# Two chunks of attention's output in one bank, two banks for the state's increment, and expert loads issued in parts

## The chip, the cores and the metric

The kernel runs on one core of one Trainium2 chip. A core has a matrix engine (PE), a vector engine (DVE), a scalar engine (ACT), a general engine (POOL) and an engine that issues loads and stores (SP); each works through its own queue in order, and semaphores tie them together. The metric is the device time of one execution in microseconds (us). Matrix products land in the banks of PSUM; DVE and ACT read them from there.

## The reference

Three layers follow one another for 2 sequences of 768 tokens, all in fp32:

```python
for t in range(S):                                   # attention: 8 heads of 64
    state = gamma * state + einsum('bhd,bhe->bhde', k[:, :, t], v[:, :, t])
    y[:, :, t] = scale * einsum('bhd,bhde->bhe', q[:, :, t], state)
# a feed-forward layer, 512 -> 1024 -> 512
h = maximum(x @ w_in, 0)
c = sum over k in 0..2 of conv_w[k] * h shifted by k - 1 tokens
x = (h * sigmoid(c)) @ w_out
# mixture of experts: 8 experts, one for each token
e = argmax(x @ w_gate) or, where sigmoid(x @ w_local) >= 0.5, the expert of the token before
out = softmax(x @ w_gate)[e] * (maximum(x @ w1[e], 0) @ w2[e])
```

The weights `w_in`, `conv_w` and `w_out` arrive as 64-bit words and are narrowed on the chip.

## The kernel before

**Attention** works on pairs of heads (8 of them, `Head`) and chunks of 128 tokens (6 for each pair), 48 iterations in one loop (lines 427 to 450). In iteration i, `scores(i)` issues PE's product of k and q (L282, bank `s`, two of them) and DVE's multiplication with the decay mask (L284, `at`). Then `output(i - 2)` issues, for an older chunk: PE's `inc`, k transposed times v (L290, bank `i`, one of them); DVE's update of the state from it, in two halves (L295 for the first chunk of a head, L297 for the others, `st`); PE's result `y` (bank `y`, two of them) from two products with `at` (L300) and one with the state that the chunk before left (L302); and ACT's copy of `y` to its high part (L304). The low part, y minus high part, is DVE's (L305); it is returned as a function and issued one iteration later. High and low part are what later products read (`xT`), since a product in fp32 is made of three (`mm3`, lines 133 to 135).

Beside it run generators that `advance()` moves on once an iteration. `convert` narrows and splits one piece of 512 columns of `w_in` or `w_out`; its part `narrow` issues DVE's L149 and L150, ACT's L151, and two steps later POOL's addition L153. The number that a generator yields is the number of iterations until it goes on. ACT's L174 and POOL's or DVE's L176 then split the narrowed piece. `prepare` gets the next head ready: ACT copies q into `qz` (L253) and v into `vz` (L277), POOL scales q (L256). From iteration 25 on the loop also issues slices of `ffn_in` (L133 to L135, `h_ps`), and `hidden` (L350 to L363) follows each of its eight blocks.

The pools of this stage hold eight tiles, each in a bank of its own: `lg` one, `s` two, `i` one, `y` two, and one each for the weights' transposes and `h_ps`. The tile in bank `lg` is called `idle` until the logits begin: `keep_busy` lets PE write there before any data has come.

**The feed-forward layer** goes on with `ffn_in` for both sequences and `ffn_out`, which stores each tile of 128 tokens to `xs` in DRAM (L491, issued by SP). For the second sequence it does so in 20 units (lines 771 to 783), two or four of them for a tile; between them stand steps of the routing (`route`, `tables`) and the first loads of the experts.

**The experts** begin with `experts` (line 934). `fetch(j, which)` loads one expert's `w1` or `w2`, 2 MB in four parts, into `r` (L698); the expert's number is read by SP from `ei`. `fetch_q` does the same for a group of four quarter tiles, one part for each of four experts (L708, `qc` and `qs1l`). `gather` lets POOL collect the 128 tokens of one tile from `xs` (L727); the first two of these read only the tiles that were stored by unit 12, and the rest comes from `LAST`. `cut` splits the loaded weights on ACT (L717) and DVE (L718), and `begin_x` transposes the gathered tokens on PE (L813).

Of the kernel before, what the change touches and what calls it, by code (L numbers as in the profile page):

```python
# [9 lines left out]
F32 = mybir.dt.float32  # L10
F32R = mybir.dt.float32r
I32 = mybir.dt.int32
U32 = mybir.dt.uint32
AF = mybir.ActivationFunctionType
# [9 lines left out]
P = 128  # L24
CH = 128
# [66 lines left out]
def tile_kernel(ctx, tc, cat, cst, qT, kT, kN, vN, w_in, conv_w, w_out, wg, w1, w2, out):  # L92
    nc = tc.nc
    te, ve, se, po, sy = nc.tensor, nc.vector, nc.scalar, nc.gpsimd, nc.sync
    ctx.enter_context(tc.manual_schedule())

    def pool(name, bufs, stack=ctx, **kw):
        return stack.enter_context(tc.tile_pool(name=name, bufs=bufs, reuse_waits="tile", **kw))
# [16 lines left out]
    ps1 = pool("ps1", 2, ps_stack, space=PSUM)  # L115
# [30 lines left out]
    def narrow(words, n):  # L146
        lo, hi = words
        a = p1.tile([P, 512], I32, tag="na", name="na", bufs=4)[:, 0:n]
        ve.tensor_scalar(out=a, in0=hi, scalar1=3, scalar2=0x3FFFFFF8, op0=ALU.logical_shift_left, op1=ALU.bitwise_and)  # L149
        ve.scalar_tensor_tensor(out=a, in0=hi, scalar=-0x40000000, in1=a, op0=ALU.bitwise_and, op1=ALU.bitwise_or)  # L150
        se.activation(out=lo, in_=lo.bitcast(U32), func=AF.Copy, scale=2.0 ** -29)  # L151
        yield 2
        po.tensor_tensor(out=a, in0=a, in1=lo, op=ALU.add)  # L153
        yield 2
        return a.bitcast(F32)
# [4 lines left out]
    def convert(src, hi, lo, m=None):  # L160
# [8 lines left out]
        while slices[0] < GATES.get(m, 0):  # L169
            yield 1  # L170
        held.append(src)
        w = yield from narrow(words, 512)
        loaded.pop()
        se.activation(out=hi, in_=w, func=AF.Copy)  # L174
# [31 lines left out]
    idle = psl.tile([P, NG, 32], F32, name="lg").rearrange("p t n -> p (t n)")  # L206
# [14 lines left out]
    class Head:  # L221
# [64 lines left out]
        def output(self, c):  # L286
            at = self.at.pop(c)
            if c + 1 < NCH:
                inc = ps1.tile([P, P], F32, tag="i", name="inc", bufs=1)
                te.matmul(inc, self.kv[:, 0, c, :], self.kv[:, 1, c, :], start=True, stop=True)  # L290
                old, new = self.st[c % 2], self.st[(c + 1) % 2]
                for j in range(2):
                    pj = slice(64 * j, 64 * j + 64)
                    if c == 0:
                        ve.tensor_copy(out=new[pj, pj], in_=inc[pj, pj])  # L295
                    else:
                        ve.scalar_tensor_tensor(out=new[pj, pj], in0=old[pj, pj], scalar=self.g[j] ** CH, in1=inc[pj, pj], op0=ALU.mult, op1=ALU.add)  # L297
            y = ps1.tile([P, CH], F32, tag="y", name="y")
            for j in range(2):
                te.matmul(y, vz[:, c, j, :], at[:, j, :], start=(j == 0), stop=(c == 0 and j == 1))  # L300
            if c > 0:
                te.matmul(y, self.st[c % 2], self.q1[:, c, :], start=False, stop=True)  # L302
            hi, lo = (self.x[:, i, c * CH:(c + 1) * CH] for i in range(2))
            se.activation(out=hi, in_=y, func=AF.Copy)  # L304
            return lambda: ve.tensor_tensor(out=lo, in0=y, in1=hi.bitcast(F32), op=ALU.subtract)  # L305

# [93 lines left out]
    parts = [(w_in[:, i, j:j + 512], wi_hi[:, i, j:j + 512], wi_lo[:, i, j:j + 512]) for j in (0, 512) for i in range(4)]  # L400
# [26 lines left out]
    for i in range(len(seq) + LOOK):  # L427
        if i < len(seq):
            p, c = seq[i]
# [12 lines left out]
        if i >= LOOK:  # L442
            p, c = seq[i - LOOK]
# [30 lines left out]
    def ffn_out(b, t, ms):  # L474

        ts = slice(t * P, (t + 1) * P)
        if ms[0] == 0:
            OUT[b, t] = psb.tile([P, DM], F32, tag="x2", name="x2_ps")
        ps = OUT[b, t]
        for m in ms:  # L480
            g = hg[b, m]
            mm3(ps, g[:, 0, ts], g[:, 1, ts], wo_hi[:, m, :], wo_lo[:, m, :], m == 0, m == 7)
        if ms[-1] == 7:
            if b == B - 1 and t >= NG - 2:
                xn = xpool[0].tile([P, DM], F32, name=f"xl{t}", bufs=1)
                LAST.append(xn)
            else:
                xn = rt.tile([P, DM], F32, name="xn", bufs=2)
            se.activation(out=xn, in_=OUT.pop((b, t)), func=AF.Copy)
            r = b * S + t * P  # L490
            sy.dma_start(out=xs[r:r + P, :], in_=xn)  # L491
# [179 lines left out]
    QSLOT = ["c4", "s1l"]  # L671
    ncut, nq = [0], [0]
    W, QW = {}, {}

    def home(tag):
        return big if tag[0] == "s" else ws if tag == "c4" else wx

    def expert_at(n):
        return sy.value_load(ei[0:1, 0, n:n + 1], min_val=0, max_val=E - 1)

    def raw(lane, which):
        if (lane, which) not in RAW:
            RAW[lane, which] = (wx if lane and which else ws).tile([P, 4, 1024], F32, name=f"r{lane}{which}")
        return RAW[lane, which]

    def fetch(j, which):

        src = (w1, w2)[which].rearrange("e p a n -> e p (a n)")
        kw = {}
        if j == 0:  # L690
            src = src[0]
        else:
            src = src[bass.ds(expert_at(j), 1)].rearrange("o p n -> (o p) n")
            if j > 1:
                kw = dict(cond=sy.value_load(ei[0:1, 1, j:j + 1], min_val=0, max_val=1), cond_hint=True)
        dst = raw(j % 2, which)
        for i in range(4):
            sy.dma_start(out=dst[:, i, :], in_=src[:, i * 1024:(i + 1) * 1024], **kw)  # L698

    def fetch_q(g, which, i):  # L700

        tag = QSLOT[nq[0] % 2]
        nq[0] += 1
        QW[g, which, i] = w = home(tag).tile([P, 4, 1024], F32, tag=tag, name="q" + tag)
        src = (w1, w2)[which].rearrange("e p a n -> e p (a n)")
        for u in range(4):
            one_e = src[bass.ds(expert_at(NTILE + 4 * g + u), 1)].rearrange("o p n -> (o p) n")
            sy.dma_start(out=w[:, u, :], in_=one_e[:, i * 1024:(i + 1) * 1024])  # L708

# [13 lines left out]
    def gather(j, n=NT):  # L723

        X[j] = xg = xpool[0].tile([P, DM], F32, name="xg")
        po.memset(xg, 0.0)
        return po.indirect_dma_start(out=xg, out_offset=None, in_=xs[0:n], in_offset=bass.IndirectOffsetOnAxis(ap=it[:, j:j + 1], axis=0),  # L727
                                     bounds_check=n - 1, oob_is_err=False)
# [43 lines left out]
    for n, (t, ms) in enumerate(units, 1):  # L772
        ffn_out(1, t, ms)
        for step in STEPS.get(n, ()):
            next(step, done)
        if n == 8:
            fetch(1, 0)
        if n in (10, 14):
            cut(0, 0, n // 14)
        if n == 13:  # L780
            fetch_q(0, 0, 0)
            for j in range(2):
                gather(j, NT - 2 * P)
    p2_stack.close()
    q_stack.close()
    lg_stack.close()
# [276 lines left out]
```

## Time and profile before

| | us |
|---|---|
| median of 3 runs | 431.09 |
| lowest and highest | 430.42, 433.47 |
| the profiled execution | 429.99 |
| its span, first to last instruction | 428.2 |

| engine | busy us | share of the span |
|---|---|---|
| PE | 407.2 | 95% |
| DVE | 289.5 | 68% |
| ACT | 259.1 | 61% |
| POOL | 90.8 | 21% |

The profile is one execution. A group of instructions has a line number, the engine, the operation, what it writes and reads, its shape and count; then its busy time in us and the mean length of one in ns; then the idle time of its engine just before its instructions, with what ended that idle time. PEld is PE's loading of weights, which runs ahead of the products. An entry in order of time starts with its start and its length in us. The ends of PE's products are modelled, because they are pipelined.

### The profile page before, as it was taken

The page shows a single profiled execution, that of the slowest core. Times are in us where ns is not written, and L with a number is a line of the kernel's source. Part 1 is how long each engine was busy: PE and PEld are TensorE (multiplying, and loading weights), DVE is VectorE, ACT ScalarE, POOL GpSimd, SP SyncE. Part 2 cuts the span into 40 slices and gives each one's busy share as a digit, 9 for nine tenths or more (in the row PEclk, how much of TensorE's full clock was granted, in tenths as well). Part 3 has the DMA queues.
Part 4 walks back from the last instruction along what each step waited for, and adds up shares of the span by engine and source line. Part 5 has one row for each costly group of instructions (what it writes and reads, how often), then busy time and mean ns, then how long its engine had stood idle before and what let it go on. Part 6 is the DMA issues. An engine that isn't in the chain of part 4 may idle for free.

```text
span 428.2 us, 7291 instructions
## 1 busy us (share of the span) xinstructions
PE 407.2 (95%) x2412; PEld 328.1 (77%) x2412; DVE 289.5 (68%) x518; ACT 259.1 (61%) x429; POOL 90.8 (21%) x92
## 2 busy tenths in 40 slices
PE   8798899999999999999999999999999999999992
PEld 7697898888898778988768876767748676776881
DVE  4588879877976350477889058968663796858650
ACT  2677777658765212566704176869555786958560
POOL 5156655121110000000000330305212132111210
PEclk9899999999999999999999999999999999999997
DMA  7969773321000101000297799999979999684001
GB/s 232 389 229 392 280 248 104 100 59 41 2 0 2 49 27 48 26 0 2 64 377 277 280 342 373 346 413 410 396 285 338 404 375 366 248 280 186 25 22 51
DMA packets 27324, 86.59 MB, mean 202 GB/s; under 512 B 3598, under 2 KB 4622, under 8 KB 27280
## 3 DMA queue, kind: packets, MB, share of 16 engines
q1 hardware_dynamic: 25200, 79.76, 50.7%
q0 software_dynamic: 2080, 6.29, 3.8%
q8 instruction: 21, 0.34, 0.3%
q14 instruction: 23, 0.19, 0.1%
HBM read 105.18 MB, written 6.55 MB: 261 GB/s over the span
## 4 chain that ended last, share of the span: by engine, by line
PE 40%; issue 26%; DMA 16%; DVE 11%; ACT 3%; POOL 2%; SPq 1%; POOLq 0%; DVEq 0%; ACTq 0%
DMA out_dram<-yo,it 14%; PE h_ps L133 6%; PE h_ps L134 5%; PE h_ps L135 5%; PE x_ps L133 4%; PE y L300 3%; PE x_ps L135 3%; PE x_ps L134 3%; PE s_ps L282 3%; PE wc_ps L193 2%; PE inc L290 2%; DMA kq<-in_qT_dram 2%; PE lg L344 1%; PE y L302 1%; DVE cc L353 1%
## 5 line engine op out<-in xcount | busy, mean ns | idle before, releaser
L133 PE MATMUL h_ps<-xT,wih 128*128 128x384 f32 x128 | 46.6, 364 | 0.0
L353 DVE SCALAR_TENSOR_TENSOR cc<-h,cw,cc 128x768 f32<-128x768 f32 x32 | 34.3, 1072 | 16.8 <-ACT cc L350 16.7
L863 POOL DMA_INDIRECT out_dram<-yo,it x13 | 16.7, 1282 | 135.2 <-ACT yo L862 135.2
L727 POOL DMA_INDIRECT xg<-xs,it x13 | 18.8, 1443 | 120.8 <-DMA qc<-in_w_dram 112.2
L134 PE MATMUL h_ps<-xT,wih 128*128 128x384 f32 x128 | 43.1, 336 | 0.0
L135 PE MATMUL h_ps<-xT,wil 128*128 128x384 f32 x128 | 43.0, 336 | 0.0
L133 PE MATMUL x_ps<-woh,hg 128*128 128x512 f32 x96 | 38.5, 401 | 0.0
L134 PE MATMUL x_ps<-wol,hg 128*128 128x512 f32 x96 | 37.5, 391 | 0.0
L135 PE MATMUL x_ps<-woh,hg 128*128 128x512 f32 x96 | 37.5, 390 | 0.0
L718 DVE TENSOR_TENSOR ws0l<-r,ws0l 128x1024 fp32r<-128x1024 f32 x22 | 26.0, 1222 | 15.9 <-ACT ws0l L717 15.8
L300 PE MATMUL y<-at,vz 128*128 128x128 f32 x192 | 31.2, 285 | 1.8 <-ACT vz L277 0.9
L153 POOL TENSOR_TENSOR na<-na,raw 128x512 int32<-128x512 int32 (+1 forms) x17 | 21.2, 1250 | 49.3 <-ACT raw L151 19.3
L718 DVE TENSOR_TENSOR ws0h<-r,ws0h 128x1024 fp32r<-128x1024 f32 x22 | 26.0, 1222 | 8.3 <-ACT ws0h L717 6.1
L718 DVE TENSOR_TENSOR wc<-r,wc 128x1024 fp32r<-128x1024 f32 x22 | 26.0, 1221 | 8.2 <-ACT wc L717 8.2
L717 ACT ACTIVATE ws0l<-r 128x1024 fp32r<-128x1024 f32 x22 | 22.1, 1052 | 13.7 <-PE y L135 13.7
L282 PE MATMUL s_ps<-qz,kq 128*128 128x256 f32 x96 | 29.1, 386 | 1.0 <-DVE qz L251 1.0
L718 DVE TENSOR_TENSOR ws1h<-r,ws1h 128x1024 fp32r<-128x1024 f32 x22 | 26.0, 1222 | 6.0 <-ACT ws1h L717 4.0
L300 PEld LDWEIGHTS y<-at,vz 128*128 128x128 f32 x192 | 25.9, 195 | 4.3 <-DVE xT L305 2.3
L717 ACT ACTIVATE wc<-r 128x1024 fp32r<-128x1024 f32 x22 | 22.1, 1054 | 11.5 <-PE g L135 11.5
L284 DVE TENSOR_TENSOR at<-s_ps,ca 128x256 f32<-128x256 f32 x48 | 20.2, 420 | 12.3 <-PE s_ps L282 12.2
L133 PEld LDWEIGHTS h_ps<-xT,wih 128*128 128x128 f32 x128 | 24.1, 189 | 3.1 <-issue 1.8
L304 ACT ACTIVATE xT<-y 128x128 fp32r<-128x128 f32 x48 | 13.2, 274 | 20.9 <-PE y L302 19.0
(231 smaller groups left out, 1035.0 us busy)
## 6 DMA issues: line engine op xcount, KB each, us to landing
r<-in_w_dram SPq DMA_DIRECT2D x88, 512.0 KB
qc<-in_w_dram SPq DMA_DIRECT2D x32, 512.0 KB
qs1l<-in_w_dram SPq DMA_DIRECT2D x32, 512.0 KB
raw<-in_w_in_dram SPq DMA_DIRECT2D x8, 512.0 KB
raw<-in_w_out_dram SPq DMA_DIRECT2D x8, 512.0 KB
kq<-in_qT_dram SPq DMA_DIRECT2D x7, 384.0 KB
kq<-in_kT_dram SPq DMA_DIRECT2D x7, 384.0 KB
kv<-in_vN_dram SPq DMA_DIRECT2D x7, 384.0 KB
```

What stands on the lines that cost most here:

```text
L133: te.matmul(ps, lhi, rhi, start=first, stop=False)
L134: te.matmul(ps, lhi, rlo, start=False, stop=False)
L135: te.matmul(ps, llo, rhi, start=False, stop=last)
L153: po.tensor_tensor(out=a, in0=a, in1=lo, op=ALU.add)
L282: te.matmul(ps, self.kq[:, 0, tok], self.qz[:, :, tok], start=True, stop=True)
L284: ve.tensor_tensor(out=self.at[c], in0=ps, in1=self.dm, op=ALU.mult)
L300: te.matmul(y, vz[:, c, j, :], at[:, j, :], start=(j == 0), stop=(c == 0 and j == 1))
L353: ve.scalar_tensor_tensor(out=cc, in0=h[:, i:i + S], scalar=cw[:, m, i:i + 1], in1=cc, op0=ALU.mult, op1=ALU.add)
L717: se.activation(out=w[:, 0, h, :], in_=r, func=AF.Copy)
L718: ve.tensor_tensor(out=w[:, 1, h, :], in0=r, in1=w[:, 0, h, :].bitcast(F32), op=ALU.subtract)
L727: return po.indirect_dma_start(out=xg, out_offset=None, in_=xs[0:n], in_offset=bass.IndirectOffsetOnAxis(ap=it[:, j:j + 1], axis=0), bound ...
L863: po.indirect_dma_start(out=out, out_offset=bass.IndirectOffsetOnAxis(ap=it[:, j:j + 1], axis=0), in_=yo, in_offset=None, bounds_check=NT ...
```

## The change

Attention's `y` becomes a tile for two chunks. The even chunk writes the first half and returns; the odd one writes the second half, and ACT's and DVE's cuts are then made once for both, 256 columns each. There are still two such banks. The increment `inc` of odd chunks goes to the `idle` bank, that of even chunks to bank `i` as before. In `narrow`, ACT's instruction is issued right after L149, and DVE's second one (L150) an iteration later than the first; the POOL addition stays two iterations after the first. `fetch` and `fetch_q` take the parts to load as an argument: the load of the second tile's `w1` is issued as two parts after unit 8 and two after unit 12 (before: four after unit 8), and the first quarter load as three parts after unit 13, behind the first two gathers, and one after unit 16 (before: four after unit 13, ahead of the gathers in the program).

```diff
@@ narrow
         ve.tensor_scalar(out=a, in0=hi, scalar1=3, scalar2=0x3FFFFFF8, op0=ALU.logical_shift_left, op1=ALU.bitwise_and)
+        se.activation(out=lo, in_=lo.bitcast(U32), func=AF.Copy, scale=2.0 ** -29)
+        yield 1
         ve.scalar_tensor_tensor(out=a, in0=hi, scalar=-0x40000000, in1=a, op0=ALU.bitwise_and, op1=ALU.bitwise_or)
-        se.activation(out=lo, in_=lo.bitcast(U32), func=AF.Copy, scale=2.0 ** -29)
-        yield 2
+        yield 1
         po.tensor_tensor(out=a, in0=a, in1=lo, op=ALU.add)
@@ Head.output
-                inc = ps1.tile([P, P], F32, tag="i", name="inc", bufs=1)
+                inc = idle[:, 0:P] if c % 2 else ps1.tile([P, P], F32, tag="i", name="inc", bufs=1)
...
-            y = ps1.tile([P, CH], F32, tag="y", name="y")
+            if c % 2 == 0:
+                self.y = ps1.tile([P, 2, CH], F32, tag="y", name="y")
+            y = self.y[:, c % 2, :]
...
-            hi, lo = (self.x[:, i, c * CH:(c + 1) * CH] for i in range(2))
+            if c % 2 == 0:
+                return None
+            y = self.y.rearrange("p c t -> p (c t)")
+            hi, lo = (self.x[:, i, (c - 1) * CH:(c + 1) * CH] for i in range(2))
             se.activation(out=hi, in_=y, func=AF.Copy)
             return lambda: ve.tensor_tensor(out=lo, in0=y, in1=hi.bitcast(F32), op=ALU.subtract)
@@ fetch, fetch_q
-    def fetch(j, which):
+    def fetch(j, which, parts=range(4)):
...
-        for i in range(4):
+        for i in parts:
...
-    def fetch_q(g, which, i):
+    def fetch_q(g, which, i, parts=range(4)):
...
-        for u in range(4):
+        for u in parts:
@@ the units of the second sequence
-        if n == 8:
-            fetch(1, 0)
+        if n in (8, 12):
+            fetch(1, 0, range(2) if n == 8 else range(2, 4))
         if n in (10, 14):
             cut(0, 0, n // 14)
         if n == 13:
-            fetch_q(0, 0, 0)
             for j in range(2):
                 gather(j, NT - 2 * P)
+        if n in (13, 16):
+            fetch_q(0, 0, 0, range(3) if n == 13 else range(3, 4))
```

## Rows read from the trace of the kernel before

**Rows 1.** The page, part 1: busy us, share of the span, instructions.

```profile
PE 407.2 (95%) x2412; PEld 328.1 (77%) x2412; DVE 289.5 (68%) x518; ACT 259.1 (61%) x429; POOL 90.8 (21%) x92
```

**Rows 2.** Busy time by stage: from:to, length, engines' busy us, clock, DMA.

```profile
18.00:93.00 75.00, 70.32 (x484) 63.67 (x483) 63.17 (x195) 54.54 (x135) 36.05 (x27) 1.00 0.63 217
93.00:133.00 40.00, 40.00 (x285) 36.47 (x285) 33.42 (x41) 28.45 (x53) 5.87 (x5) 1.00 0.05 15
...
246.00:428.00 182.00, 172.74 (x952) 123.81 (x950) 120.98 (x119) 122.06 (x160) 38.40 (x34) 0.99 0.75 286
```

**Rows 3.** Groups of 18 to 93 us: PE and its weight loader, attention's products.

```profile
L300 PE MATMUL y<-at,vz 128*128 128x128 f32 x177 | 28.2, 281 | 0.9 <-DVE xT L305 0.6
...
L300 PEld LDWEIGHTS y<-at,vz 128*128 128x128 f32 x176 | 23.2, 191 | 3.2 <-DVE xT L305 2.3 <-issue 0.5
...
L290 PE MATMUL inc<-kv 128*128 128x128 f32 x72 | 14.3, 281 | 3.3 <-DVE st L297 2.8 <-DVE st L295 0.5
...
L290 PEld LDWEIGHTS inc<-kv 128*128 128x128 f32 x72 | 13.0, 189 | 7.2 <-issue 3.4 <-PE s_ps L282 1.7 <-PE h_ps L135 0.4
```

**Rows 4.** In order of time, 31.7 to 39.6 us: start, length, instruction.

```profile
31.76 1.59 DVE L149 TENSOR_SCALAR na<-raw 128x512 int32<-128x512 int32 x1
...
31.86 0.38 PE L290 MATMUL inc<-kv 128*128 128x128 f32 x2
...
32.53 0.39 PE L302 MATMUL y<-kq,st 128*128 128x128 f32 x2
...
33.39 0.69 DVE L150 SCALAR_TENSOR_TENSOR na<-raw,na 128x512 int32<-128x512 int32 x1
...
34.21 1.29 POOL L153 TENSOR_TENSOR na<-na,raw 128x512 int32<-128x512 int32 x1 [0.77 <-ACT wih L174]
...
34.91 0.46 PE L290 MATMUL inc<-kv 128*128 128x128 f32 x2 [1.56 <-DVE st L297]
...
38.94 0.62 ACT L174 ACTIVATE wih<-na 128x512 fp32r<-128x512 f32 x1
```

**Rows 5.** Groups of 18 to 93 us: the cuts and what they are costed by.

```profile
L284 DVE TENSOR_TENSOR at<-s_ps,ca 128x256 f32<-128x256 f32 x42 | 17.6, 420 | 8.1 <-PE s_ps L282 8.0
...
L305 DVE TENSOR_TENSOR xT<-y,xT 128x128 fp32r<-128x128 f32 x45 | 13.1, 290 | 1.6 <-ACT xT L304 0.5
...
L304 ACT ACTIVATE xT<-y 128x128 fp32r<-128x128 f32 x45 | 12.4, 275 | 20.4 <-PE y L302 18.6 <-PE y L300 1.5
...
L150 DVE SCALAR_TENSOR_TENSOR na<-raw,na 128x512 int32<-128x512 int32 (+1 forms) x14 | 9.2, 656 | 0.5
...
L189 ACT ACTIVATE wt<-wt_ps 128x512 f32<-128x512 f32 x2 | 1.2, 590 | 0.0
```

**Rows 6.** Busy time of 69 to 78 us; L353 in 18 to 93 us and overall.

```profile
69.00:78.00 9.00, 8.58 (x58) 7.35 (x57) 8.75 (x22) 5.73 (x14) 3.23 (x3) 1.00 0.34 94
...
L353 DVE SCALAR_TENSOR_TENSOR cc<-h,cw,cc 128x768 f32<-128x768 f32 x3 | 3.9, 1300 | 0.3 <-ACT cc L350 0.3
...
L353 DVE SCALAR_TENSOR_TENSOR cc<-h,cw,cc 128x768 f32<-128x768 f32 x32 | 34.3, 1072 | 16.8 <-ACT cc L350 16.7
```

**Rows 7.** In order of time, 226 to 251 us: SP's issues and who waits.

```profile
226.80 1.95 SPq L698 DMA_DIRECT2D r<-in_w_dram  x4
230.72 0.34 SPq L491 DMA_DIRECT2D xs<-xn  x1
231.85 4.08 SPq L708 DMA_DIRECT2D qc<-in_w_dram  x4
...
236.59 1.21 POOL L727 DMA_INDIRECT xg<-xs,it  x1 [112.17 <-DMA qc<-in_w_dram]
...
242.59 1.13 PE L813 MATMUL tp<-cs,xg 128*128 128x128 f32 x8 [0.29 <-DMA xg<-xs,it]
...
248.72 2.00 ACT L717 ACTIVATE ws1h<-r 128x1024 fp32r<-128x1024 f32 x2
```

More of the change, by code (lines that the diff above doesn't have):

```diff
@@ L696, in fetch @@
         dst = raw(j % 2, which)
-        for i in range(4):
+        for i in parts:
             sy.dma_start(out=dst[:, i, :], in_=src[:, i * 1024:(i + 1) * 1024], **kw)
-    def fetch_q(g, which, i):
-        tag = QSLOT[nq[0] % 2]
-        nq[0] += 1
-        QW[g, which, i] = w = home(tag).tile([P, 4, 1024], F32, tag=tag, name="q" + tag)
+    def fetch_q(g, which, i, parts=range(4)):
+        if (g, which, i) not in QW:
+            tag = QSLOT[nq[0] % 2]
+            nq[0] += 1
+            QW[g, which, i] = home(tag).tile([P, 4, 1024], F32, tag=tag, name="q" + tag)
+        w = QW[g, which, i]
         src = (w1, w2)[which].rearrange("e p a n -> e p (a n)")
-        for u in range(4):
+        for u in parts:
             one_e = src[bass.ds(expert_at(NTILE + 4 * g + u), 1)].rearrange("o p n -> (o p) n")
```

## The prediction

> **What bounds the kernel now.** I read the page's part 1 first, then the busy time by stage, then, inside the one stage that the change touches most, the grouped instructions and the order of time.
>
> Part 1 says that the PE is busy for 95% of the span and the next engine, DVE, for 68% [rows 1]. An average hides stages, so the second view cuts the span where the kernel changes its work [rows 2]. From 18 to 93 us (attention, with the weight conversion and the first slices of `ffn_in` between the chunks) PE is busy for 70.3 of 75.0 us, and here DVE is nearly as full, 63.2 of 75.0. From 93 to 133 us PE has no gap at all, 40.00 of 40.00. From 246 us on (experts) PE is busy for 172.7 of 182. So PE sets the pace in every stage, and a microsecond that attention gives back reaches the end, as long as PE stays the bound there. The place where PE has gaps that this change can touch is 18 to 93 us.
>
> Which gaps? The groups of that stretch with their idle time [rows 3]: before `inc` (L290) PE stood still for 3.3 us, 2.8 of it until DVE's `st` (L297); before `y` (L300) for 0.9 us, mostly until DVE's `xT` (L305). The weight loader, which runs ahead of the matmuls, stood still for 7.2 and 3.2 us before the same two. PE's ends are modelled, so the true loss lies between: at least 3.3 + 0.9 = 4.2 us, at most 7.2 + 3.2 = 10.4 us. I take the middle, 5.25 for `inc` and 2.05 for `y`, together 7.3 us.
>
> The mechanism of the largest one can be read in order of time [rows 4]. PE writes `inc` of one chunk at 31.86 us. DVE should then read it into `st`, but it is busy with a piece of weight conversion: L149 from 31.76 us for 1.59 us and right behind it L150 for 0.69 us. There is one bank for `inc`, so the next `inc` cannot be written until DVE has read the last, and PE begins it at 34.91 us after 1.56 us of idling that ended with `st`.
>
> **The change part by part.**
>
> *Two banks for `inc`.* The next `inc` no longer waits for `st` of the last. The wait is not gone: the third product of `y` (L302) reads that `st`, and it stands behind `inc` and two products of `y`. From `inc` at 31.86 to L302 at 32.53 us is 0.67 us [rows 4]. So each wait shrinks by 0.67 us, and those shorter than that vanish. The largest falls from 1.56 to 0.9 us.
>
> *L150 an iteration later.* DVE now reads `inc` between L149 and L150, which takes another 0.69 us off that wait: 0.2 us. But L150 is then in the way of the next chunk's `st`. So between 0.2 us (all of it absorbed) and 0.9 us (all of it paid a chunk later) stays; I take 0.55. The other waits for L297 add up to 2.8 - 1.56 = 1.24 us [rows 3, 4]; by the same rule between 0 and 1.24 - 0.67 = 0.57 stays, and I take 0.3. L151 goes to ACT in the same place as before and costs nothing new. The POOL addition L153, which needs L150, comes one iteration behind it and not two; behind L153 POOL has the scaling of `q1` for the next head, which is read a head later. What hides the delay is the distance to its reader: L153 of this piece runs from 34.21 to 35.50 us and ACT's L174, which needs it, only at 38.94 us, 3.4 us later [rows 4]. Without that cover it is rival E.
>
> *One bank for two chunks of `y`.* The bank that a pair writes was last used two pairs ago, so its readers have two iterations instead of one; I count the 2.05 us of L300 as gone. The two cuts also become half as many: ACT's L304 takes 275 ns for 128 columns and L189, also from PSUM, 590 ns for 512 columns, so 256 columns cost about 380 ns by the straight line between them (bounds: 275, the same as 128, and 550, two of them); DVE's L305 takes 290 ns and L284, from PSUM with 256 columns, 420 ns [rows 5]. That is 2 x 275 - 380 = 170 ns less for ACT and 2 x 290 - 420 = 160 ns less for DVE for each of 24 pairs, 4.1 and 3.8 us in all, of which about 22 pairs, 3.5 us of DVE, lie in this stretch. PE does not wait for these cuts by themselves, so this counts only as room on DVE. The cut of an even chunk comes up to one iteration later; its reader, `ffn_in`, takes most of `xT` from heads that are long done, and I cost that at nothing.
>
> So of 7.3 us, 7.3 - 0.55 - 0.3 = 6.45 us could go. I do not count all of it. DVE has 75.0 - 63.2 = 11.8 us of idle time in this stretch to catch up in. With 6.45 us less span and 3.5 us less work it has 68.55 - 59.7 = 8.85, a quarter less. From 69 to 78 us it is already busy for 8.75 of 9.00 us [rows 6]; there PE can only gain what DVE's queue gives. So I count three quarters: 4.8 us. It is an estimate from these rows; its bounds are 1.8 (rival B) and 7.3.
>
> *The expert loads in parts.* The store of the fourth tile of `xs` is issued by SP at 230.72 us, behind four parts of `r` (the whole 2 MB tile) that began at 226.80 us; the first gather, on POOL, needs that store and begins only at 236.59 us; PE begins on the gathered tile at 242.59 us after idling 0.29 us for it [rows 7]. With two parts moved behind the store the store has 1 MB less ahead of it and the gather can start earlier, by at most the 5.9 us from the issue to its start. PE gains the 0.29 us it waited, no more: 0.3. The moved loads: two parts of `r` are issued some 4 to 5 us later, with one more read of the expert's number each way, and are first cut by ACT at 248.72 us [rows 7], over 10 us behind their issue. The fourth part of `qc` goes behind the next store, with as much time before its use in the first group. SP has the issues spread over a stretch in which it otherwise waits for stores. If that cover were gone, ACT's cut would wait and PE after it; nothing in these rows points there. Bounds of this part: 0 and 0.7.
>
> **Sum.** 4.8 + 0.3 = 5.1 us. The profiled execution took 429.99 us (span 428.2), 1.1 us less than the median of the runs, 431.09. So 424.9 us for such an execution, and 431.09 - 5.1 = 426.0 us as the median. "Faster" means below 426.8 us and "slower" above 435.4 us: 1% is about what a measurement of this kernel can tell from no change.
>
> **Rivals.**
>
> A, the forecast: 426.0 us.
>
> B, the wait only moves to L302 and DVE is the bound behind it. Then each `inc` wait gains its 0.67 us at most: 3.3 - 0.9 - 0.57 = 1.8 us, and PE meets the time saved on `y` again at the next `st`. For it: DVE at 8.75 of 9.00 us [rows 6]. Against it: before 69 us DVE has idle time between its backlogs. With 0.3 from the loads: 2.1 us, 429.0 us.
>
> C, every wait for `inc` and `y` vanishes: 7.3 + 0.3 = 7.6 us, 423.5 us. For it: the split of L149 and L150 and the lighter cuts both work on the backlog that makes the waits. The upper bound of rows 3, 10.4 us, lies behind it.
>
> D, L150 gets slower because it now runs beside POOL. Today it follows L149, which has already sat out POOL's instruction (1.59 us where L150 takes 0.69). On its own it can meet one. Rows for it: L353, also two tensors from SBUF, takes 1300 ns here, where POOL is busy, against 1072 ns over the whole run [rows 6]. Against it: L150's mean of 14 is 656 ns, as if never stretched [rows 5]. If each of the 13 full pieces in the stretch waited out one POOL addition of 1.29 us [rows 4], DVE would have 16.8 us more to do and 11.8 + 3.5 = 15.3 us of room; it would be the bound, nothing would be gained, and 1.5 us lost: 432.6 us. It begins to eat the gain when DVE's room is used, at some 0.4 us per piece. The Trainium skill states such a rule ("SBUF — State Buffer", section "Who interferes with whom"): a DVE instruction with two SBUF inputs contends with a GpSimd instruction that reads SBUF, and the order of issue decides who blocks. By that rule L150 could be held for a whole POOL instruction, which is the price just worked out; L353's rows agree in part, a stretch of a fifth and not a block.
>
> E, slower: ACT is held by POOL. If L150, now behind a chunk's work, made L153 so late that ACT's L174 had to wait for it, everything behind L174 in ACT's queue (the cuts of `y`, the copies of `qz` and `vz` for the next head) would wait and PE after them. Price: up to 1.29 us for each of 13 pieces, 16.8 us, so 431.1 - 5.1 + 16.8 = 442.8 us; it turns the sign from 0.4 us per piece. Against it stand the 3.4 us between L153's end and L174 [rows 4]: L150 would have to come that much later, and one iteration is well under half of it.
>
> **How the numbers follow.** A 0.48, B 0.24, C 0.12, D 0.09, E 0.07. The forecast is A. Its own spread, about 1.5 us from the three-quarter factor, puts a sixth of it above 426.8: faster 0.40 + 0.12 = 0.52; same 0.08 + 0.24 + 0.06 of D = 0.38; slower 0.07 of E and 0.03 of D = 0.10. The range holds A, B and most of C, 422.8 to 430.2 us; it leaves out the far end of C, D and E.
>
> **What would show each step.** In the profile after: `inc` (L290) without idle time for DVE, and a smaller idle time before the third product of `y`, on `st`; no idle time before L300 on `xT`; 24 cuts of 256 columns on each of ACT and DVE at about 380 and 420 ns; L150 still near 0.66 us (longer: D); no wait of ACT on L153 (there: E); the end of attention some 5 us earlier, and the shift kept at 133 and 246 us; POOL's first gather some 3 us sooner than the shift alone makes it, and PE without a wait for it. The prediction is wrong if DVE's idle time in the stretch nears zero (B), or if the shift of attention shrinks in a later stage because a load or DVE, not PE, ends last there.

## The result, and the profile after

| | before | after |
|---|---|---|
| median of 6 runs, us | 430.75 | 424.28 |
| lowest and highest | 429.39, 433.47 | 423.65, 425.27 |
| the profiled execution, us | 429.99 | 423.86 |
| its span | 428.2 | 422.0 |

The ratio is 0.9866, with a 95% interval of 0.9838 to 0.9895: 5.8 us less, between 4.5 and 7.0.

The first view is the page's part 1 of the kernel after, which answers [rows 1]; the second is the busy time by stage (from:to, length, busy us of PE, PEld, DVE, ACT and POOL, clock, DMA share, GB/s), which answers [rows 2].

```profile
PE 405.7 (96%) x2412; PEld 329.0 (78%) x2412; DVE 290.1 (69%) x494; ACT 256.5 (61%) x405; POOL 93.6 (22%) x92
...
18.00:93.00 75.00, 73.51 (x519) 68.99 (x518) 68.46 (x176) 55.42 (x119) 39.85 (x28) 1.00 0.63 219
```

PE is now busy for 73.5 of the 75 us from 18 to 93 us, where it was 70.3, and does 519 products there instead of 484. DVE has gone up with it, from 63.2 to 68.5 us.

The groups of the same stretch answer [rows 3, 5] (line, engine, operation, tiles, count; busy us and mean ns; idle before them and what ended it). In the kernel after, `inc` is L291, in both its banks (`inc` and `lg`), the first two products of `y` are L303, the third L305, `st` is L298, ACT's cut L310, DVE's L311, and the second half of `narrow` on DVE is L152.

```profile
L303 PE MATMUL y<-at,vz 128*128 128x128 f32 x172 | 26.2, 275 | 0.0
...
L305 PE MATMUL y<-kq,st 128*128 128x128 f32 x73 | 15.1, 287 | 1.4 <-DVE st L298 0.9 <-issue 0.3
L152 DVE SCALAR_TENSOR_TENSOR na<-raw,na 128x512 int32<-128x512 int32 (+1 forms) x15 | 12.2, 812 | 0.1
L149 DVE TENSOR_SCALAR na<-raw 128x512 int32<-128x512 int32 (+1 forms) x15 | 11.1, 739 | 0.1
...
L305 PEld LDWEIGHTS y<-kq,st 128*128 128x128 f32 x72 | 10.9, 191 | 3.0 <-DVE st L298 2.4 <-issue 0.4
L311 DVE TENSOR_TENSOR xT<-y,xT 128x256 fp32r<-128x256 f32 x23 | 9.8, 425 | 0.7
L310 ACT ACTIVATE xT<-y 128x256 fp32r<-128x256 f32 x22 | 8.4, 383 | 16.0 <-PE y L305 16.0
L291 PE MATMUL inc<-kv 128*128 128x128 f32 x42 | 8.1, 274 | 0.0
...
L291 PE MATMUL lg<-kv 128*128 128x128 f32 x28 | 5.4, 274 | 0.0
...
L175 ACT ACTIVATE woh<-na 128x512 fp32r<-128x512 f32 x5 | 3.2, 631 | 0.8 <-POOL na L154 0.7
```

The idle time before `inc` (3.3 us) and before the first two products of `y` (0.9) is gone. One wait is left, before the third product, on `st`: 1.4 us of PE, 3.0 of the loader; before, there was none at that place in this stretch (L302 there):

```profile
L302 PE MATMUL y<-kq,st 128*128 128x128 f32 x76 | 14.7, 275 | 0.0
```

In order of time the same piece of the weight conversion as in [rows 4] (start and length in us):

```profile
29.33 0.38 PE L291 MATMUL inc<-kv 128*128 128x128 f32 x2
29.40 1.14 DVE L149 TENSOR_SCALAR na<-raw 128x512 int32<-128x512 int32 x1
...
30.66 0.38 PE L291 MATMUL lg<-kv 128*128 128x128 f32 x2
...
31.01 0.46 DVE L298 SCALAR_TENSOR_TENSOR st<-st,inc 64x64 f32<-64x64 f32 x2
31.52 0.30 PEld L305 LDWEIGHTS y<-kq,st 128*128 128x128 f32 x2 [0.23 <-DVE st L298]
...
31.84 0.68 DVE L152 SCALAR_TENSOR_TENSOR na<-raw,na 128x512 int32<-128x512 int32 x1
...
32.77 0.46 DVE L298 SCALAR_TENSOR_TENSOR st<-st,lg 64x64 f32<-64x64 f32 x2
...
33.29 0.49 PE L305 MATMUL y<-kq,st 128*128 128x128 f32 x2 [0.18 <-DVE st L298]
```

L149 is again in `st`'s way, but the next `inc` is written into the other bank at 30.66 us, before `st` has read the first at 31.01. Where PE stood still for 1.56 us, its loader now waits 0.23.

**Where the time went, stage by stage.** PE issues the same 2412 products in the same order in both kernels and in all those below, so stages can be cut at the same products and their lengths compared, whatever came earlier. I cut at the 86th (third product of a `y`; 19.31 us before, 17.76 after), the 651st (in `ffn_in`; 105.13 and 99.04), the 1432nd (the last of `ffn_out`; 241.91 and 235.85), the 1434th (the second of the first `begin_x`), the 1531st and the last, each at its start, and call the stages attention, feed-forward, first gather, first tiles and experts.

| us | before 86th | attention | feed-forward | first gather | first tiles | experts |
|---|---|---|---|---|---|---|
| before | 19.31 | 85.82 | 136.78 | 0.86 | 16.24 | 160.50 |
| after | 17.76 | 81.29 | 136.80 | 0.34 | 16.24 | 160.49 |
| gain | 1.55 | 4.53 | -0.02 | 0.52 | 0.00 | 0.01 |

Between the 86th and the last product the change is worth 4.53 + 0.52 = 5.05 us, and nothing of it is lost in the later stages. Behind the last product come only the last output copies and stores: 8.71 us before and 9.07 after. That end took 8.69 to 9.50 us in the fourteen profiles of this document, so I count its 0.36 us neither way. The 1.55 us of the start are another matter; the last section comes to them.

### The profile page after: what moved, and what is told of

It reads as the page before. It is cut to its first block, busy times and chain, and to the rows that moved or that the text cites. A ratio compares the mean times of both kernels' runs of the same rounds, so it can differ in the third digit from the quotient of the medians.

```text
span 422.0 us, 7240 instructions
## 1 busy us (share of the span) xinstructions
PE 405.7 (96%) x2412; PEld 329.0 (78%) x2412; DVE 290.1 (69%) x494; ACT 256.5 (61%) x405; POOL 93.6 (22%) x92
## 4 chain that ended last, share of the span: by engine, by line
PE 41%; issue 26%; DMA 17%; DVE 9%; POOL 2%; ACT 2%; SPq 1%; POOLq 0%; DVEq 0%
DMA out_dram<-yo,it 15%; PE h_ps L133 6%; PE h_ps L134 5%; PE h_ps L135 5%; PE x_ps L133 4%; PE x_ps L134 3%; PE x_ps L135 3%; PE y L303 3%; PE s_ps L283 3%; PE y L305 2%; PE wc_ps L194 2%; DMA kq<-in_qT_dram 2%; PE lg L350 1%; DVE at L285 1%; POOL xg L735 1%
## 5 line engine op out<-in xcount | busy, mean ns | idle before, releaser
L154 POOL TENSOR_TENSOR na<-na,raw 128x512 int32<-128x512 int32 (+1 forms) x17 | 23.0, 1354 | 50.6 <-DVE na L152 25.8
L303 PE MATMUL y<-at,vz 128*128 128x128 f32 x192 | 29.6, 276 | 1.2 <-ACT vz L278 1.2
L303 PEld LDWEIGHTS y<-at,vz 128*128 128x128 f32 x192 | 25.9, 192 | 1.8 <-ACT vz L278 1.4
L495 ACT ACTIVATE xn<-x_ps 128x512 f32<-128x512 f32 x10 | 6.0, 598 | 32.8 <-PE x_ps L135 15.5
```

## The experiments

All were compared with the kernel before. "Attention" and "first gather" are the stages above in one profiled execution of each; the ratio is that of the timed runs, with its 95% interval. The attention stage repeats closely: kernels with the same attention code differ by at most 0.02 us in it (before and only_loads, after and no_loads, no_narrow and q_late and two_two). The later stages do not repeat like that.

| kernel | median us | ratio | attention | first gather | first tiles | experts |
|---|---|---|---|---|---|---|
| only_inc | 429.75 | 0.9991 (0.9964 to 1.0018) | 85.81 | 1.53 | 16.25 | 160.15 |
| only_ypair | 427.0 | 0.9926 (0.9901 to 0.9951) | 83.08 | 2.47 | 16.27 | 162.55 |
| only_narrow | 429.61 | 0.9984 (0.9953 to 1.0014) | 85.53 | 1.89 | 16.28 | 161.77 |
| only_loads | 429.57 | 0.9979 (0.9954 to 1.0004) | 85.84 | 1.21 | 17.02 | 160.15 |
| no_inc | 427.29 | 0.9925 (0.9896 to 0.9954) | 83.18 | 0.34 | 16.52 | 160.53 |
| no_ypair | 428.9 | 0.9962 (0.9931 to 0.9992) | 85.41 | 0.34 | 16.50 | 160.94 |
| no_narrow | 424.7 | 0.9848 (0.9811 to 0.9885) | 80.19 | 1.17 | 16.20 | 160.61 |
| no_loads | 425.72 | 0.9876 (0.9838 to 0.9914) | 81.30 | 1.69 | 16.31 | 161.75 |
| two_cuts | 426.12 | 0.9891 (0.9852 to 0.9929) | 81.86 | 0.34 | 16.23 | 160.23 |
| q_late | 427.31 | 0.9930 (0.9902 to 0.9958) | 80.18 | 0.34 | 17.74 | 160.04 |
| q_late_st | 427.82 | 0.9935 (0.9903 to 0.9967) | 80.78 | 0.34 | 22.19 | 159.25 |
| two_two | 423.13 | 0.9859 (0.9823 to 0.9895) | 80.18 | 0.34 | 16.57 | 160.44 |

The longest entries of the last column go with PE waiting for quarter loads (`qc`, `qs1l`) some 55 us into that stage: the loader's waits there are 2.8 us before and 2.9 after, but 5.5 in only_ypair, 4.8 in only_narrow and 4.2 in no_loads. Before and only_inc issue the same loads and have the short wait, so I put it down to no part of the change.

### The second bank for `inc`, alone and taken away

only_inc is the kernel before with one line of the change; no_inc is the kernel after with that line undone.

```diff
-                inc = ps1.tile([P, P], F32, tag="i", name="inc", bufs=1)
+                inc = idle[:, 0:P] if c % 2 else ps1.tile([P, P], F32, tag="i", name="inc", bufs=1)
```

> The kernel before with one part of the change: inc of odd chunks goes to the second bank. My theory: the wait moves from inc to the third product of y and shrinks by 0.67 us each time; with L149 and L150 still back to back 0.9 and 0.6 us of the larger waits stay, so 5.25 - 1.5 = 3.75, of which three quarters: 2.8 us faster. Rival (the wait only moves and DVE sets the pace): 1.8 us faster or less, and the idle time before the third product of y on st above 2 us. In the trace: no idle time before inc on st in either case.

> The changed kernel with one bank for inc; the pair's bank for y, the later L150 and the loads in parts stay. New theory: PE stops at inc again, idle there 2.5 to 3.5 us as before; attention keeps the 2.5 us of the y bank; 2 to 3 us slower than the changed kernel, 3.5 to 4.5 us under the kernel before. Rival (the second bank is worth nothing, as it was alone): no difference from the changed kernel.

Alone it gave nothing: attention 85.81 us against 85.82. The groups of only_inc from 18 to 93 us, and the backlog of [rows 4] in it in order of time:

```profile
L300 PE MATMUL y<-at,vz 128*128 128x128 f32 x172 | 27.5, 283 | 4.5 <-DVE xT L305 4.2
...
L290 PE MATMUL inc<-kv 128*128 128x128 f32 x42 | 8.1, 274 | 0.0
```

```profile
31.15 0.39 PE L290 MATMUL lg<-kv 128*128 128x128 f32 x2
31.35 0.69 DVE L150 SCALAR_TENSOR_TENSOR na<-raw,na 128x512 int32<-128x512 int32 x1
31.96 0.42 DVE L284 TENSOR_TENSOR at<-s_ps,ca 128x256 f32<-128x256 f32 x1
32.29 0.46 DVE L297 SCALAR_TENSOR_TENSOR st<-st,inc 64x64 f32<-64x64 f32 x2
32.78 0.29 DVE L305 TENSOR_TENSOR xT<-y,xT 128x128 fp32r<-128x128 f32 x1
...
33.22 0.68 PE L300 MATMUL y<-at,vz 128*128 128x128 f32 x4 [1.68 <-DVE xT L305]
```

PE passes `inc` without a stop and stands still at the very next instruction, the first product of `y`: its bank comes free with DVE's low part L305, which is queued behind `st`. The 3.3 + 0.9 us of [rows 3] have become 0.0 + 4.5. Product by product, only_inc gains 1.80 us on the kernel before at this `inc` and loses 1.82 at this `y`.

With the other parts there (no_inc against after) the same line is worth 83.18 - 81.29 = 1.89 us, and in no_inc the wait before `inc` is back, 3.3 us.

### One bank for two chunks of `y`, alone, taken away, and with its cuts not merged

```diff
-            y = ps1.tile([P, CH], F32, tag="y", name="y")
+            if c % 2 == 0:
+                self.y = ps1.tile([P, 2, CH], F32, tag="y", name="y")
+            y = self.y[:, c % 2, :]
...
+            if c % 2 == 0:
+                return None
+            y = self.y.rearrange("p c t -> p (c t)")
```

> The kernel before with one part of the change: y of two chunks in one bank, cut at once. My theory: the waits of y for DVE's low part (0.9 us on PE, 3.2 on its weight loader) go, three quarters of their middle is kept: 1.5 us faster. Rival: the time saved is lost again at the next inc, which still has one bank: no difference, and the idle time before inc grows from 3.3 us by as much as that before y falls.

> The changed kernel with y again in a bank for each chunk; the second bank for inc, the later L150 and the loads in parts stay. New theory, after the four parts alone: DVE is late, and PE stops at the first of three places that need it: inc, then y's first product (DVE's low part of two chunks before must be out of the bank), then y's third product. Taking the first away alone moves the wait 0.2 us on. So the attention stage gains nothing to speak of over the kernel before, idle time before y's first product is 3 to 5 us, and the time is 1 us or less under the kernel before. Rival (each part adds its own gain, as I predicted): the loss against the changed kernel is that of the y bank alone, 2 to 3 us, so some 3 to 4 us under the kernel before.

The groups of 18 to 93 us, of only_ypair (two rows) and of no_ypair (one):

```profile
L302 PE MATMUL y<-at,vz 128*128 128x128 f32 x176 | 26.8, 275 | 0.0
...
L290 PE MATMUL inc<-kv 128*128 128x128 f32 x72 | 14.5, 283 | 3.3 <-DVE st L297 2.3 <-DVE st L295 0.9
```

```profile
L301 PE MATMUL y<-at,vz 128*128 128x128 f32 x176 | 28.4, 284 | 4.0 <-DVE xT L306 3.9
```

Alone it takes 2.74 us off attention, and the wait before `inc` stays as it was, 3.3 us. Taken away from the kernel after, it costs 85.41 - 81.29 = 4.12 us, and the wait is at `y` again, as in only_inc. So the two banks are worth nothing or 2.7 us one at a time and 85.82 - 80.19 = 5.63 us together (no_narrow, below, has both and L150 in its old place).

two_cuts keeps the shared bank, but ACT and DVE each cut it in two instructions of 128 columns:

```diff
-            se.activation(out=hi, in_=y, func=AF.Copy)
+            for u in range(2):
+                us = slice(u * CH, (u + 1) * CH)
+                se.activation(out=hi[:, us], in_=y[:, us], func=AF.Copy)
...
```

> The changed kernel, but y's pair is cut in two cuts of 128 columns, both after the odd chunk, on ACT and on DVE; the banks stay as in the change. If the y part pays by its banks: no difference from the changed kernel, or 0 to 0.7 us slower by the 3.8 us more of DVE work in a stage where DVE is nearly full. Rival (it pays by the shorter cuts): 1.5 to 2.5 us slower.

Attention takes 81.86 us, 0.57 more than after, where the separate banks of no_ypair cost 4.12. So most of what the part is worth comes from the bank, whose readers have two iterations instead of one, and the small rest from the fewer cuts; the timed ratios of the two kernels (0.9891 and 0.9866) can't be told apart.

### L150 an iteration later

only_narrow makes this part alone; no_narrow is the kernel after with L150 right behind L149 again.

```diff
+        se.activation(out=lo, in_=lo.bitcast(U32), func=AF.Copy, scale=2.0 ** -29)
+        yield 1
         ve.scalar_tensor_tensor(out=a, in0=hi, scalar=-0x40000000, in1=a, op0=ALU.bitwise_and, op1=ALU.bitwise_or)
-        se.activation(out=lo, in_=lo.bitcast(U32), func=AF.Copy, scale=2.0 ** -29)
-        yield 2
+        yield 1
```

> The kernel before with one part of the change: the second half of narrow on DVE (L150) an iteration later. My theory: with one bank the longest waits of inc lose 0.69 us each and a part comes back an iteration later: 0.5 to 1.0 us faster. Rival (L150 alone meets POOL's instructions and is held): L150 well above 0.7 us, no gain or up to 1.5 us slower.

> The changed kernel with L150 again right behind L149. My predicted step: the longest waits, now at y's third product, grow by up to 0.69 us each, two or three of them: 0.7 to 1.5 us slower than the changed kernel. Rival (the later L150 only pays a chunk later): no difference, the same idle time before y's third product, spread over fewer and longer waits.

Alone it helps attention by 0.29 us. Beside the two banks it hurts: 81.29 us with it, 80.19 without, 1.10 us; neither the theory of no_narrow nor its rival had that sign. The groups of no_narrow from 18 to 93 us, to be read against those of after (L305, L152 and L149 there):

```profile
L304 PE MATMUL y<-kq,st 128*128 128x128 f32 x72 | 14.2, 279 | 1.6 <-DVE st L297 1.6
L150 DVE SCALAR_TENSOR_TENSOR na<-raw,na 128x512 int32<-128x512 int32 (+1 forms) x15 | 9.9, 659 | 0.5
L149 DVE TENSOR_SCALAR na<-raw 128x512 int32<-128x512 int32 (+1 forms) x15 | 8.8, 589 | 0.1
```

For the same 15 pieces DVE spends 12.2 + 11.1 = 23.3 us after and 18.7 without this part: 4.6 us more. Of the 14 full second halves 12 still take 0.68 or 0.69 us; two take 2.12 and 1.68. The longest of them in order of time, in the kernel after:

```profile
57.22 1.83 POOL L257 TENSOR_TENSOR kq<-kq,ca 128x768 f32<-128x768 f32 x1 [1.95 <-DMA kv<-in_vN_dram]
57.48 2.12 DVE L152 SCALAR_TENSOR_TENSOR na<-raw,na 128x512 int32<-128x512 int32 x1
```

POOL's instruction begins 0.26 us earlier and ends at 59.05; DVE's ends 0.55 us after it. The Trainium skill ("SBUF — State Buffer", section "Who interferes with whom") says that a DVE instruction with two SBUF inputs contends with a POOL (GpSimd) instruction that reads SBUF, and that the order of issue decides which of them is blocked. This row agrees. In all, three of the 14 full pieces began while a POOL instruction ran, with 1.57, 1.14 and 0.09 us of it still to go, and each ended 0.55 to 0.59 us after it; no POOL instruction ran beside the other 11. The other half of the 4.6 us is L149, of which six of 14 took over 0.8 us and four of 14 without this part. Those six, too, had a POOL instruction beside them and ended 0.28 or 0.29 us after it.

Against no_narrow, product by product, the kernel after gains 0.63 us in one step, at the third product of 31.52 us shown above, behind the long L149, and 0.35 at another, behind the L149 of 1.58 us: there the part does what it is said to do. A further 0.24 us comes at the last product of the stage, where no_narrow waits for ACT. It loses 0.2 to 0.45 us in each of seven others, all at the third product of `y`, 2.3 us in all. The first of them is the next chunk's (the last rows of that fence): L152, 0.68 us as ever, is now ahead of its `st`, and PE begins at 33.29 us after idling for `st`. The fourth comes right behind the piece of 2.12 us; before the other six L152 had its ordinary 0.68 or 0.69 us. So most of the loss goes with the new place in DVE's queue and little with longer pieces, though no run separates the two.

### The expert loads

only_loads makes this part alone; no_loads undoes it in the kernel after. Its core:

```diff
-        if n == 8:
-            fetch(1, 0)
+        if n in (8, 12):
+            fetch(1, 0, range(2) if n == 8 else range(2, 4))
...
-            fetch_q(0, 0, 0)
...
+        if n in (13, 16):
+            fetch_q(0, 0, 0, range(3) if n == 13 else range(3, 4))
```

> The kernel before with one part of the change: the expert loads in parts. My theory: only PE's idle time before the first transposes of the gathered tokens goes, 0.3 us, too little to be told from no change; attention is as before. Rival: the loads in parts give over 1 us, by the experts' first loads or gathers coming earlier to something that waits.

> The changed kernel with the expert loads whole as before; the three attention parts stay. New theory: with attention faster PE comes to the first transpose of the gathered tokens sooner, but the gather's start hangs on a store behind 2 MB of loads, so PE waits there for 1 to 2 us and the gain of attention is lost by that much: 1 to 2 us slower than the changed kernel. Rival (my predicted step): 0.3 us slower, not to be told from the changed kernel.

In order of time, the kernel after:

```profile
225.78 0.86 SPq L704 DMA_DIRECT2D r<-in_w_dram  x2
227.44 2.59 SPq L716 DMA_DIRECT2D qc<-in_w_dram  x3
227.88 1.21 POOL L735 DMA_INDIRECT xg<-xs,it  x1 [109.53 <-DVE pr L671]
...
236.08 1.05 PE L822 MATMUL tp<-cs,xg 128*128 128x128 f32 x8
```

and no_loads:

```profile
225.23 4.12 SPq L714 DMA_DIRECT2D qc<-in_w_dram  x4
...
231.09 1.21 POOL L733 DMA_INDIRECT xg<-xs,it  x1 [113.35 <-DMA qc<-in_w_dram]
...
236.80 1.13 PE L819 MATMUL tp<-cs,xg 128*128 128x128 f32 x8 [1.12 <-DMA xg<-xs,it]
```

With attention as fast as after and the loads whole, the gather begins 3.2 us later and PE waits for it: the first gather stage takes 1.69 us instead of 0.34. In this pair the change's loads save 1.35 us of it. Alone (only_loads) the stage takes 1.21 us and the first tiles 17.02, no gain; the timed ratios of no_loads and of after overlap.

The theory of no_loads had the size of the wait right, but not its reason: it is not the faster attention that opens it. In all kernels here SP issues the store of the fourth tile 11.19 us ahead of the last product of `ffn_out`, so the store moves along with PE, whatever attention takes. What differs is how long the gather takes from there. Both parts of that time, in us, the second by the records of the transfers:

| kernel | loads | attention | store's issue to gather's start | gather's start to landing | first gather |
|---|---|---|---|---|---|
| before | whole | 85.82 | 5.87 | 5.86 | 0.86 |
| only_inc | whole | 85.81 | 6.99 | 5.42 | 1.53 |
| only_narrow | whole | 85.53 | 7.35 | 5.41 | 1.89 |
| only_ypair | whole | 83.08 | 7.92 | 5.42 | 2.47 |
| no_loads | whole | 81.30 | 7.00 | 5.57 | 1.69 |
| only_loads | in parts | 85.84 | 5.78 | 6.30 | 1.21 |
| no_ypair | in parts | 85.41 | 3.23 | 7.92 | 0.34 |
| after | in parts | 81.29 | 3.23 | 7.75 | 0.34 |
| no_narrow | in parts | 80.19 | 3.46 | 8.58 | 1.17 |

What the two parts have together over 11.19 us, PE waits; the stage is that wait and 0.34 us of its own, to within 0.03. With attention as slow as before, only_inc and only_narrow wait longer than before does: of five profiles with the loads whole, that of the kernel before has the shortest wait. With the loads in parts the gather begins 3.2 to 3.5 us after the store's issue instead of 5.9 to 7.9 (only_loads apart) and, with loads issued around it, takes some 2 us longer; after, it lands 0.2 us ahead of PE, and in no_narrow it does not. In only_loads the two parts ahead of the store were issued 1.8 us before it (3.8 in the kernel after), and the gather began as late as with the loads whole; what held them back was not followed up.

### Beyond the change: the loads again, and `st` ahead of the mask

In no_narrow PE waits for the gather once more (first gather 1.17 us), since it takes 8.6 us there. q_late is no_narrow with all four quarter loads behind unit 16; two_two has two of them there.

```diff
-        if n in (13, 16):
-            fetch_q(0, 0, 0, range(3) if n == 13 else range(3, 4))
+        if n == 16:
+            fetch_q(0, 0, 0)
```

> The changed kernel with two edits: L150 right behind L149 again, and all four parts of the first quarter load issued after unit 16, none after unit 13. Without the first edit's cost attention ends 1.3 us sooner (as in the run with that edit alone, where PE then waited 0.98 us for the gathered tokens). My theory: the gathers were slow, 8.6 us from start to landing, because 2.5 MB of loads ran beside them; with those later they land in 5 to 6 us, PE does not wait there, and the time is 0.8 to 1.5 us under the changed kernel. Rival: the loads are the bound from here on, what is issued later comes later, and PE waits for the same time at a later load (group 1's weights): no difference.

> The changed kernel with L150 right behind L149 again and the first quarter load as two parts after unit 13 and two after unit 16. It lies between two runs: with three and one PE waited about 1 us for the first gather, with none and four it lost 2.2 us at the transpose of the quarter tile, whose gather needs the last store, which stood behind those four parts. My theory: both waits go by what stands ahead of a store or beside a gather, so here the first wait is 0 to 0.6 us and the second 0 to 0.8 us, and the time is that of the run with three and one or 0.5 us less, 423.5 to 425 us. Rival: the second wait comes as a step, as soon as the last store meets any load in the queue: 1.5 us slower than with three and one.

q_late's first gather takes 4.3 us, with no load issued beside it, and PE doesn't wait for it. But the four loads now stand before the store of the last tile, and the next gather, of a quarter tile, pays. In order of time:

```profile
230.64 3.71 SPq L715 DMA_DIRECT2D qc<-in_w_dram  x4
...
234.98 0.33 SPq L496 DMA_DIRECT2D xs<-xl  x1
...
240.83 1.00 POOL L734 DMA_INDIRECT xg<-xs,it  x1 [10.09 <-DMA xs<-xl]
...
247.77 0.66 PE L808 MATMUL tp<-cs,xg 128*128 128x128 f32 x4 [2.26 <-DMA xg<-xs,it]
```

From that store's issue to the gather it releases 5.9 us pass. With fewer quarter loads between the last two stores it was less: 4.0 in two_two with two, 3.8 after with one (236.90 to 240.70), 2.8 before with none. The first tiles take 17.74 us, 1.5 more than after. two_two lies between (16.57) and has the lowest median, 423.13 us, but its ratio, 0.9859 (0.9823 to 0.9895), can't be told from that of no_narrow or of after. The theory of q_late was right on the first gather and missed the second: its median is 3.0 us above that of after. Its profile, 422.93 us, is the shortest of its seven executions; the other six took 426.1 to 428.0 us at a mean granted clock of 0.984 to 0.993, against 0.996 in the profile. What happened in those six is in no trace; the next kernel's profile shows one way to lose such a time ("The clock after a wait").

q_late_st issues DVE's mask product behind `st` and not ahead of it, in q_late:

```diff
-            ve.tensor_tensor(out=self.at[c], in0=ps, in1=self.dm, op=ALU.mult)
+            return lambda: ve.tensor_tensor(out=self.at[c], in0=ps, in1=self.dm, op=ALU.mult)
...
```

> As the run before, and DVE updates the state before it masks the chunk's scores (st, then the low part's turn, with the mask between). My theory: what is left of the waits, 1.6 us on PE before y's third product, is for st, and DVE reaches st 0.33 us sooner, so 0.5 to 1.2 us of it goes. Rival: the mask comes later, and PE's next scores wait for its bank: no gain or up to 1 us slower.

Attention takes 80.78 us against 80.18: no gain, a loss of 0.60, as the rival had it. From 18 to 93 us the wait before the third product does shrink, from 1.6 to 1.1 us:

```profile
L304 PE MATMUL y<-kq,st 128*128 128x128 f32 x72 | 14.3, 280 | 1.1 <-DVE st L297 1.0
```

But the mask now comes later: the loader waits 0.5 us for `at` before the scores (L282), where it waited for nothing in q_late, and the stage as a whole is longer.

## Why the prediction came out, step by step

**What bounds the kernel: right.** PE sets the pace, and what attention gave back reached the last product whole: feed-forward, first tiles and experts have the same length in both kernels.

**The sum: 5.1 us expected, 5.05 measured behind the 86th product (4.53 for attention against 4.8, 0.52 for the loads against 0.3).** That it came so close is luck: two errors inside attention's 4.8 nearly cancelled.

*Two banks for `inc`: the step failed where it said where the wait goes.* It was to move to the third product of `y` and to shrink by 0.67 us. Alone it moved 0.33 us on, to the first product, and didn't shrink. I had priced the wait before `y` as a wait of its own, 2.05 us, gone with the shared bank; but the 0.9 us that [rows 3] show there is what is left once `inc` has absorbed the same backlog. Two banks wait for one late engine, and the row of the second shows only what the first leaves of it. So the prices do not add: 0.0 and 2.74 alone, 5.63 together. With the shared bank the step came true: the third product waits on `st`, 1.4 us.

*Three quarters of what could go: the deduction was not borne out.* The two middles of [rows 3] sum to 7.3. With L150 in its old place, by the prediction's own rule 0.9 + 0.57 of them stay, and 5.83 could go; 5.63 went (no_narrow). So with L150 in its old place nearly all went, and the quarter that I held back made room, by luck, for what L150 cost. My reason for the deduction was DVE's shrinking idle time: in the same 75 us, which now hold more of the work, it fell from 11.8 to 6.5 us, and DVE still did not become the bound.

*L150 an iteration later: wrong in sign.* It was to take 0.69 us off the largest wait, and took 0.63; alone it was worth 0.29 us. For all waits it was to save 0.35 + 0.27 = 0.62 us. With the two banks it cost 1.10: the piece is paid for at the next chunk's `st`, which I had allowed for at the large backlogs only, and not at the others, where nothing is won. I also kept its length at 0.66 us from [rows 5], where it stood right behind L149; its mean became 0.81.

*The cuts: right.* 383 and 425 ns against 380 and 420. I counted them as room only; 0.57 us is what they gave (two_cuts).

*The expert loads: mechanism right, size off.* With 1 MB less ahead of the store the gather began sooner, as forecast: some 3 us sooner than the shift was expected, 2.6 came (236.59 - 227.88 = 8.7, less 6.1 of shift). Two things were mis-sized. I took the 0.29 us that PE waited in one execution [rows 7] for the wait of the kernel, and it was the shortest of five: the stage took 0.86 to 2.47 us with the loads whole. And I kept the gather's own length, which grew from 5.9 to 7.7 us, so that it landed only 0.8 us sooner than the shift. Between the two kernels the stage gave 0.52 us; only_loads gave nothing.

**Rivals.** B's picture, a wait that only moves, came true where only the bank of `inc` is doubled, but the wait went to the first product and not to the third, and the gain was 0.0 and not B's 1.8; it did not come true in the full change. C did not: 1.4 us are left at the third product. D happened in 2 of 14 pieces (2.12 and 1.68 us), far from the 13 it needed. E left a trace of 0.7 us (ACT's L175 on POOL's L154) that PE did not feel: ACT's cuts wait for PE 16.0 us in this stretch.

**Median against profile.** The medians differ by 6.5 us, the ratio gives 5.8, the stages 5.05; the interval of 4.5 to 7.0 holds it. The two profiled executions differ by 6.2 us of span: 1.55 ahead of the 86th product, 5.05 behind it, less 0.36 behind the last. The forecast of the median, 426.0 us, was 1.7 above the measured 424.28; the forecast for such an execution, 424.9, was 1.0 above 423.86.

## To carry to other kernels

When several buffers wait for the same late engine, PE's idle time is booked to the first of them in its queue, and a second buffer for that one only moves the wait to the next: walk on along the queue, name the next buffer that the late engine has to free, and price them together. A wait for a transfer, read from one execution, is one draw: the same order of issues gave 0.9 to 2.5 us here, and the row of before had the least. Write such a wait as a sum, from the issue that releases the transfer to its landing, against the time at which PE comes for it, and ask how far each part can spread. A slot "an iteration later" is not free: what an instruction meets there, on another engine too, is not in the mean it had in its old place.

## What the runs showed of the chip

**The clock at the start.** In the profiled execution of before, TensorE ran for most of 14 to 18 us at the lower of its levels, 1.2 GHz (granted clock 0.57), after 5 us in which PE was busy for 3.33; in the one of after it kept 2.4 GHz. Busy time by stage, two rows of before and two of after:

```profile
9.00:14.00 5.00, 3.33 (x23) 2.52 (x21) 2.64 (x10) 2.51 (x5) 0.74 (x1) 1.00 1.00 374
14.00:18.00 4.00, 3.16 (x14) 2.99 (x15) 1.50 (x6) 2.13 (x6) 1.54 (x1) 0.57 1.05 397
```

```profile
9.00:14.00 5.00, 3.81 (x24) 3.17 (x24) 3.18 (x11) 2.60 (x5) 1.43 (x2) 1.00 1.02 377
14.00:18.00 4.00, 3.33 (x25) 3.23 (x26) 1.96 (x7) 2.97 (x8) 1.38 (x1) 1.00 1.05 390
```

It goes with no part of the change: the profiles of only_ypair, no_ypair and two_cuts have it, those of the other nine kernels do not. What sets it off stays open; each profile is one execution.

**The clock after a wait.** In q_late_st PE waited at `tp` (L810) for the quarter gather for 4.5 us, its loader for 4.9. Busy time by stage:

```profile
246.00:249.00 3.00, 0.48 (x3) 0.06 (x1) 0.93 (x1) 1.08 (x2) 2.21 (x3) 0.99 1.03 406
249.00:256.00 7.00, 5.00 (x14) 4.10 (x15) 2.27 (x2) 2.49 (x3) 0.00 (x0) 0.52 1.01 391
256.00:262.00 6.00, 6.00 (x47) 2.92 (x46) 4.21 (x6) 4.87 (x6) 0.00 (x0) 1.00 0.56 194
```

From 249 to 256 us the granted clock was 0.52: PE had 1.2 GHz for nearly all of these 7 us, and 2.4 GHz from 256 us on. The first tiles took 22.19 us against 17.74 in q_late, 4.45 us more, though the loader's wait there is only 2.2 us longer (4.9 and 2.7): the longer wait cost about twice its own length.

**A gather beside loads.** The first gather, of 128 tokens, took 4.3 us from issue to landing in q_late, with no load issued beside it; 5.4 to 5.9 us in the five kernels with the loads whole, all four quarter loads issued ahead of it; 7.7 us after and 8.6 in no_narrow, with three quarter loads issued around it. What moves a gather ahead of a load also moves it into the company of that load.
